# Decode attention with a gated feed-forward: one ordered load queue into five 32 KB slots, in place of two queues with their own buffers

## The chip, the cores and the metric

The kernel runs on one core of a Trainium2 chip. A core has five engines that each work through their own list of instructions: TensorE (PE, matrix products, with its weight loads shown apart as PEld), VectorE (DVE), ScalarE (ACT), GpSimd (POOL) and SyncE (SP, which here only starts transfers). They meet through semaphores. Data comes from the chip's memory (HBM) into SBUF (128 partitions) through 16 DMA engines that all queues share. PE writes into PSUM, eight banks of 2 KB per partition.

The metric is device time in microseconds (us), the median over several runs. Before the change it is 385.56 us, median of 3 runs (385.26 to 386.15).

## The reference, cut to what matters

One token (x, 512 values) goes through attention over a cache of 32,768 keys and through a feed-forward block, and the two results are mixed by a scalar gate.

```
q = x @ wq                                  # 512 -> 32 heads x 128
scores = einsum("bhqd,bhkd->bhqk", q, k) * Dh**-0.5   # k, v: 8 kv heads, each for 4 q heads
p = softmax(scores)                         # over 32768 keys
a = einsum("bhqk,bhkd->bhqd", p, v).reshape(1, 1, 4096) @ wo      # 4096 -> 512
b = (silu(x @ w_gate) * (x @ w_up)) @ w_down                      # 512 -> 1792 -> 512
g = sigmoid(sum(x * gate_w))
out = g * a + (1 - g) * b
```

All inputs are bfloat16. k_cache and v_cache hold 67.1 MB each, wq and wo 4.19 MB each, the three feed-forward matrices 1.84 MB each. Each byte is used once, and 148.11 MB are read in all.

## The kernel before, in words

Keys lie in the cache as rows of 128 values. PE turns 8 tiles of 128 keys into columns (a *fill*: 8 transposes against an identity, L474, into one of three PSUM tiles `pst`), DVE copies the fill to SBUF (L722, `ktT`), and PE multiplies each of the 8 tiles with the group's 4 query columns (*scores*, L443, three fills later, into `ps_sc`). A group is one kv head: 256 tiles, 32 fills. When a group's scores are there, DVE and POOL find the maximum (L706, L314) and ACT takes exponentials (L571) into `ET`, one of three group buffers. Then PE sums the values: one matmul per tile of 128 keys with the tile of V as the weights and 4 columns of `ET` moving (*PV*, L496, 256 per group into `ps_o`).

**Loads.** K comes in 64 blocks of 1 MB: 128 partitions with 32 rows of 256 bytes each, an 8 KB run of memory per partition. SP issues them (L341) into four slots of `kbuf`; each waits until PE has transposed the block that held the slot (`s_fill`). On the same queue, x, gate_w and wq come first (L320 to L322), the feed-forward matrices follow K blocks 3, 5 and 7 (L348), and wo follows K block 40 (L351). V also comes in 64 blocks of 1 MB, on ACT's queue (L609), into eight slots of `vbuf` and, later, four in the space of wq (`wqo`). ACT issues each at a place in its own program that `v_thr` works out, between the exponentials. So two queues share the DMA engines.

**PE's order** is the list `jobs`: from group 1 on, K blocks of group g alternate with V blocks of group g-1; a K block is four times (8 transposes, 8 scores), a V block is 32 PV matmuls in a row. The feed-forward's products (L394 with a strided view of the weights, L407) and the query product (L379) are inserted by number of fill.

**The end.** The last group's PV is followed by a sum of the exponentials over partitions (L512), reciprocal, scaling, a transpose within DVE and a permutation by matmul (L747 to L756, L521), 128 matmuls with wo (L528), the mix (L758, L763), four transposes of the result into one row (L538), a cast (L772) and the store of 512 values as one row (L357).

Of the kernel before, what the change touches and what calls it, by code (L numbers as in the profile page):

```python
# [5 lines left out]
ACT = mybir.ActivationFunctionType  # L6
# [7 lines left out]
def bass_gated_mix__gqa_block_cached__swiglu_ffn__decode_kernel(  # L14
# [14 lines left out]
    Hkv = A_k_cache.shape[1]  # L29
# [3 lines left out]
    HPG = H // Hkv  # L33
    F = B_w_gate.shape[1]
    NOUT = A_wo.shape[1]
    assert DH == 128 and D % 128 == 0 and F % 128 == 0 and HPG == 4 and NOUT % 128 == 0
    assert H == 32, "wo blocked layout / permutation assumes 32 q heads of 128"
    KC = D // 128
    FC = F // 128
    OC = NOUT // 128  # L40
    G = Hkv
    assert G >= 3
    R = 32
    B = 128 * R
    assert S % B == 0
    NB = S // B
    NT = NB * R
    TPF = 8
    FPB = R // TPF
    FPG = NB * FPB  # L50
    NF = G * FPG
    TPSB = 512 // HPG
    FPSB = TPSB // TPF
    NSB = G * NT // TPSB
    assert NT % TPSB == 0 and (NT // TPSB) == 2
    NKB = 4
    NVB = NB
    NVX = 4
    NVT = NVB + NVX
    VI_EXT = NB  # L60
# [5 lines left out]
    VLAG = 3  # L66
    WOJ = H * DH // 128
    SCALE = float(DH) ** -0.5

    J_FFN = FPG + 2  # L70
    J_ACT_SG = J_FFN + 6
    J_DVE_T = J_ACT_SG + 4
    J_OUTB = J_DVE_T + 8
    J_BCOL = J_OUTB + 3
    assert J_BCOL + LAG + NST < 2 * FPG, "ffn chain must complete inside group 1"

    def sb_thr(f):
        return min(NF - 1, FPSB * f + FPSB - 1 + LAG + 1)

    def exp_thr(g):  # L80
        return sb_thr(2 * g + 1)

    act_busy = set()
    for g in range(G):
        t0 = exp_thr(g)
        for j in range(t0 + 1, t0 + 11):
            act_busy.add(j)

    def copier(j):
        if j in act_busy:  # L90
            return "D"
        return "D"

    cp_index = []
    nd = na = 0
    for j in range(NF):
        if copier(j) == "D":
            nd += 1
            cp_index.append(("D", nd))
        else:  # L100
            na += 1
            cp_index.append(("A", na))

    jobs = []
    for g in range(G):
        kj = [("K", g, b) for b in range(NB)]
        vj = [("V", g - 1, b) for b in range(NB)] if g >= 1 else []
        seq = kj[:VLAG] if g >= 1 else kj[:]
        ki = len(seq)
        vi = 0  # L110
        turn_v = True
        while ki < len(kj) or vi < len(vj):
            if turn_v and vi < len(vj):
                seq.append(vj[vi])
                vi += 1
            elif ki < len(kj):
                seq.append(kj[ki])
                ki += 1
            else:
                seq.append(vj[vi])  # L120
                vi += 1
            turn_v = not turn_v
        jobs += seq
    jobs += [("V", G - 1, b) for b in range(NB)]
    assert len(jobs) == 2 * G * NB

    NVALL = G * NB
    vslot = [0] * NVALL
    vprev = [-1] * NVALL
    _occ = {}  # L130
    for vi in range(NVALL):
        allowed = range(NVT) if vi >= VI_EXT else range(NVB)
        free = [sl for sl in allowed if sl not in _occ]
        if free:
            sl = free[0]
        else:
            sl = min(allowed, key=lambda x: _occ[x])
            vprev[vi] = _occ[sl]
        vslot[vi] = sl
        _occ[sl] = vi  # L140

    with ExitStack() as es:
        def S_(name):
            return es.enter_context(nc.semaphore(name))

        sem_k_load = [S_(f"s_k_load{i}") for i in range(NKB)]
        sem_v_load = [S_(f"s_v_load{i}") for i in range(NVT)]
        sem_fill = S_("s_fill")
        sem_kt_free = S_("s_kt_free")
        sem_v_free = S_("s_v_free")  # L150
        sem_cp_d = S_("s_cp_d")
        sem_cp_a = S_("s_cp_a")
        sem_ld_x = S_("s_ld_x")
        sem_ld_wq = S_("s_ld_wq")
        sem_ld_wf = S_("s_ld_wf")
        sem_ld_wo = S_("s_ld_wo")
        sem_out = S_("s_out")
        sem_const = S_("s_const")
# [4 lines left out]
        sem_dve_pm = S_("s_dve_pm")  # L163
        sem_pe_x = S_("s_pe_x")
        sem_pe_q = S_("s_pe_q")
        sem_pe_h = S_("s_pe_h")
# [4 lines left out]
        sem_pe_fin = S_("s_pe_fin")  # L171
        sem_dve_x = S_("s_dve_x")
        sem_dve_prod = S_("s_dve_prod")
        sem_dve_gpart = S_("s_dve_gpart")
        sem_dve_qT = S_("s_dve_qT")
        sem_dve_t1 = S_("s_dve_t1")
        sem_dve_tT = S_("s_dve_tT")
        sem_dve_bcol = S_("s_dve_bcol")
        sem_pmax = S_("s_pmax")
        sem_dve_esum2 = S_("s_dve_esum2")  # L180
        sem_dve_rS = S_("s_dve_rS")
        sem_dve_oT1 = S_("s_dve_oT1")
        sem_dve_oT2 = S_("s_dve_oT2")
        sem_dve_O2 = S_("s_dve_O2")
        sem_dve_diff = S_("s_dve_diff")
        sem_dve_res = S_("s_dve_res")
        sem_dve_row = S_("s_dve_row")
        sem_act_g = S_("s_act_g")
        sem_act_sg = S_("s_act_sg")
# [611 lines left out]
```

## Time and profile before

| what | value |
|---|---|
| median of the runs (lowest, highest) | 385.56 us (385.26, 386.15) |
| span of the profiled execution, first to last instruction | 384.1 us |
| mean granted clock of TensorE | 0.746 |
| PE busy; weight loads | 298.7 us (78%); 293.3 us (76%), 6583 instructions each |
| DVE busy | 188.1 us (49%) |
| ACT busy | 30.4 us (8%) |
| read from HBM | 148.11 MB, 386 GB/s over the span |
| K and everything else on SP's queue | 81.01 MB, 51.0% of the 16 DMA engines |
| V on ACT's queue | 67.11 MB, 42.7% |
| instruction fetches on queue q8 | 51 packets, 0.84 MB, 0.9% |

The profiled execution spans 384.1 us, 1.5 us below the median of the runs; a run also has what lies around the instructions. The page gives busy time by engine, the same in 40 slices of 9.6 us, the DMA queues, the chain of work that ended last, and the costliest groups of instructions. In the profile, "issue" as the releaser of a wait means that the engine waited for nothing that the profile shows: no semaphore, no operand. Queue q1 is SP's, q10 ACT's, and q8 carries the instructions of the engines themselves from memory.

### The profile page before, as it was taken

What the parts mean: (1) busy time and instruction counts of PE and PEld (TensorE: products, weight loads), DVE (VectorE), ACT (ScalarE), POOL (GpSimd) and SP (SyncE); (2) the same over time, 40 slices, a digit from 0 to 9 for tenths busy, and PEclk for the clock granted to TensorE, in tenths of its full rate; (3) what the DMA queues carried; (4) which work ended last, traced back from release to release, by engine and by line L of the source; (5) the groups of instructions that cost most, each with busy time, mean ns of one, the idle gap of its engine ahead of it and who ended that gap; (6) DMA issues with size and microseconds to landing.
All of it is one profiled execution on the core that took longest, in us unless ns stands there. A gap on an engine that the chain in (4) does not pass through costs nothing.

```text
span 384.1 us, 14171 instructions
## 1 busy us (share of the span) xinstructions
PE 298.7 (78%) x6583; PEld 293.3 (76%) x6583; DVE 188.1 (49%) x305; ACT 30.4 (8%) x142; POOL 4.5 (1%) x19
## 2 busy tenths in 40 slices
PE   0592644899779797989997893278898888888895
PEld 0592644899779797989997893278898888887885
DVE  0291523427447464765575553155447653755502
ACT  1000000140003100300030002000003000300030
POOL 0000000000000000000000000000000000000000
PEclk9996656659787868595669885588668887788855
DMA  7999999989998999999999999999999999999810
GB/s 307 398 422 418 420 423 418 385 339 426 414 417 315 381 417 418 418 419 413 418 417 419 415 434 421 411 420 418 416 419 420 411 418 418 404 422 417 357 72 2
DMA packets 19215, 149.01 MB, mean 388 GB/s; under 512 B 2131, under 2 KB 2134, under 8 KB 2134
## 3 DMA queue, kind: packets, MB, share of 16 engines
q1 hardware_dynamic: 9942, 81.01, 51.0%
q10 hardware_dynamic: 9216, 67.11, 42.7%
q8 instruction: 51, 0.84, 0.9%
q14 instruction: 6, 0.05, 0.0%
HBM read 148.11 MB, written 0.00 MB: 386 GB/s over the span
## 4 chain that ended last, share of the span: by engine, by line
PE 46%; DMA 40%; issue 13%; DVE 1%; ACT 0%; SPq 0%; POOLq 0%; POOL 0%; ACTq 0%
DMA kbuf<-in_A_k_cache_dram 36%; PE pst L474 26%; PE ps_o L496 8%; PE ps_sc L443 7%; DMA wqo<-in_A_wq_dram 3%; PE ps_m L394 2%; PE ps_m L528 1%; PE ps_m L379 1%; PE ps_m L407 0%; ACT ET L571 0%; DVE ktT L722 0%; DVE res_row L772 0%; DVE pmaxf L706 0%; PE pst L538 0%; PE pst L512 0%
## 5 line engine op out<-in xcount | busy, mean ns | idle before, releaser
L722 DVE COPY ktT<-pst 128x1024 bf16<-128x1024 bf16 x256 | 172.9, 691 | 160.1 <-PE pst L474 159.0
L474 PE MATMUL pst<-ident,kbuf 128*128 128x128 bf16 x2048 | 208.2, 264 | 52.1 <-DMA kbuf<-in_A_k_cache_dram 49.8
L474 PEld LDWEIGHTS pst<-ident,kbuf 128*128 128x128 bf16 x2048 | 157.3, 118 | 55.5 <-DMA kbuf<-in_A_k_cache_dram 52.0
L443 PE MATMUL ps_sc<-qT,ktT 128*128 128x4 bf16 x2048 | 95.2, 168 | 2.8 <-issue 2.5
L443 PEld LDWEIGHTS ps_sc<-qT,ktT 128*128 128x128 bf16 x2048 | 92.0, 105 | 3.3 <-issue 2.7
L496 PE MATMUL ps_o<-ET,vbuf 128*128 128x4 bf16 x1408 | 42.7, 168 | 7.9 <-issue 7.9
L496 PEld LDWEIGHTS ps_o<-ET,vbuf 128*128 128x128 bf16 x1408 | 40.0, 98 | 8.4 <-issue 8.3
L561 ACT ACTIVATE nbias<-gmax 128x4 f32<-128x4 f32 x8 | 1.6, 206 | 316.3 <-POOL gmax L314 316.3
L571 ACT ACTIVATE ET<-ps_sc,nbias 128x128 bf16<-128x128 f32 x64 | 22.5, 377 | 0.2
L496 PE MATMUL ps_o<-ET,wqo 128*128 128x4 bf16 x640 | 19.0, 168 | 3.0 <-issue 2.3
L496 PEld LDWEIGHTS ps_o<-ET,wqo 128*128 128x128 bf16 x640 | 18.0, 98 | 3.2 <-issue 2.4
L571 ACT ACTIVATION_READ_ACCUMULATOR ET<-ps_sc,nbias 128x1 f32 x64 | 13.8, 216 | 0.0
L379 PE MATMUL ps_m<-xT,wqo 128*128 128x1 bf16 x128 | 3.5, 165 | 11.0 <-DMA wqo<-in_A_wq_dram 11.0
L379 PEld LDWEIGHTS ps_m<-xT,wqo 128*128 128x128 bf16 x128 | 3.5, 104 | 11.1 <-issue 11.1
L706 DVE TENSOR_REDUCE pmaxf<-ps_sc 128x4 f32<-128x512 f32 x16 | 10.9, 681 | 0.4 <-PE ps_sc L443 0.4
L314 POOL PARTITION_ALL_REDUCE gmax<-pmax x8 | 3.0, 373 | 340.2 <-DVE pmax L710 340.2
L394 PE MATMUL ps_m<-xT,wfo 128*128 128x1 bf16 x112 | 6.9, 198 | 0.0
L394 PEld LDWEIGHTS ps_m<-xT,wfo 128*128 128x128 bf16 x112 | 6.8, 166 | 0.0
L661 DVE TENSOR_SCALAR kq<-kf 128x1 f32<-128x1 f32 x3 | 0.5, 153 | 8.6 <-POOL kf L300 8.5
L528 PE MATMUL ps_m<-O,wfo 128*128 128x1 bf16 x128 | 3.7, 165 | 0.4 <-DVE O L756 0.3
L528 PEld LDWEIGHTS ps_m<-O,wfo 128*128 128x128 bf16 x128 | 3.6, 104 | 0.6 <-DVE O L756 0.4
L747 DVE RECIPROCAL rS<-pst 128x32 f32<-128x32 f32 x1 | 0.4, 359 | 6.3 <-PE pst L512 6.3
(50 smaller groups left out, 19.7 us busy)
## 6 DMA issues: line engine op xcount, KB each, us to landing
kbuf<-in_A_k_cache_dram SPq DMA_DIRECT2D x64, 1024.0 KB, 16.1
vbuf<-in_A_v_cache_dram ACTq DMA_DIRECT2D x44, 1024.0 KB, 23.9
wqo<-in_A_v_cache_dram ACTq DMA_DIRECT2D x20, 1024.0 KB, 22.4
wqo<-in_A_wq_dram SPq DMA_DIRECT2D x1, 4096.0 KB, 12.3
wfo<-in_A_wo_dram SPq DMA_DIRECT2D x1, 4096.0 KB, 28.2
wfo<-in_B_w_gate_dram SPq DMA_DIRECT2D x1, 1792.0 KB, 27.2
wfo<-in_B_w_up_dram SPq DMA_DIRECT2D x1, 1792.0 KB, 23.8
wfo<-in_B_w_down_dram SPq DMA_DIRECT2D x1, 1792.0 KB, 36.2
```

The costliest lines, as they stand in the source:

```text
L314: pool.partition_all_reduce(gmax[:, g, :], pmax[:, g, :], 128, ReduceOp.max).then_inc(sem_gmax, 1)
L379: ins = pe.matmul(ps_m[:, M_Q0 + h : M_Q0 + h + 1], wq_v[:, c, h * DH : (h + 1) * DH], xT[:, c : c + 1], start=(c == 0), stop=(c == KC - 1),)
L394: ins = pe.matmul(ps_m[:, base + j : base + j + 1], wt[:, c, :].rearrange("d (p j) -> d j p", j=FC)[:, j, :], xT[:, c : c + 1], start=(c = ...
L443: ins = pe.matmul(bank[:, col : col + HPG], ktT[:, slot, t * 128 : (t + 1) * 128], qT[:, g * HPG : (g + 1) * HPG], start=True, stop=True,)
L474: ins = pe.transpose(stb[:, t * 128 : (t + 1) * 128], kbuf[:, slot, r, :], ident[:, :],)
L496: ins = pe.matmul(ps_o[:, g * HPG : (g + 1) * HPG], vsl[:, r, :], ET[:, g % NEG, :, n], start=(n == 0), stop=(n == NT - 1),)
L528: ins = pe.matmul(ps_m[:, M_A0 + oc : M_A0 + oc + 1], wo_v[:, j, oc * 128 : (oc + 1) * 128], O2[:, j : j + 1], start=(j == 0), stop=(j == ...
L561: act.activation(nbias[:, g, :], gmax[:, g, :], ACT.Copy, scale=-SCALE).then_inc(sem_nbias, 1)
L571: act.activation(ET[:, g % NEG, h, bk * TPSB : (bk + 1) * TPSB], sc[:, h, :], ACT.Exp, bias=nbias[:, g, h : h + 1], scale=SCALE, accum_out ...
L661: dchain(dve.tensor_scalar(kq[:, i : i + 1], kf[:, :], thr, None, op0=ALU.is_ge))
L706: dve.tensor_reduce(pmaxf[:, f, :], sc, AX.X, ALU.max).then_inc(sem_pmax, 1)
L722: dve.tensor_copy(ktT[:, j % NKT, :], pst[j % NST][:, :]).then_inc(sem_cp_d, 1)
```

## The change

All large loads now go through SP's queue alone, in the order of one list, `stream`: wq, K half 0 of group 0, w_gate and w_up, K half 1, w_down, K half 0 of group 1 and V half 0 of group 0, and so on in pairs, V being one group behind; the last two V halves and wo close the list. An entry takes one of five slots of 32 KB per partition (`ring`), and is issued when the entry five places before it has been used up. K and V now come in halves of a group, 4 MB at a time, with one 32 KB run of memory per partition. The last V half is cut into pieces of 2 MB, 1 MB and two of 512 KB, wo into pieces of the same sizes. x and gate_w are loaded as columns by two small transfers on ACT's queue, and ACT issues nothing else.

PE follows `pe_work`. From K half 1 of group 1 on, each K half is worked together with the V half before it in sixteen equal parts: 8 transposes, 8 scores, 8 PV. The gate's sum over partitions is a matmul in place of a POOL reduction. At the end, the sum of the exponentials stands before the last V half. The wo products run over its 32 row blocks outermost and four result columns inside, with a strided view of wo, into four PSUM banks, so they can begin with the first piece. The result is mixed in one DVE operation and stored from 128 partitions with 4 values each. The four transposes, the cast and two of the DVE steps are gone.

The core of the diff:

```diff
-    jobs = []
-    for g in range(G):
-        kj = [("K", g, b) for b in range(NB)]
-        vj = [("V", g - 1, b) for b in range(NB)] if g >= 1 else []
...
+    RH = S // 256
+    SLOT = RH * DH
+    NSLOT = 5
+    FPH = RH // TPF
+    V_LAST = (64, 32, 16, 16)
+    WO_CUT = (16, 8, 4, 4)
+    stream = [("wq",), ("K", 0, 0), ("F1",), ("K", 0, 1), ("F2",)]
+    for g in range(1, G):
+        for hf in range(2):
+            stream += [("K", g, hf), ("V", g - 1, hf)]
+    stream += [("V", G - 1, 0), ("V", G - 1, 1), ("wo",)]
...
-                for kind, g, b in [j for j in jobs if j[0] == "K"]:
-                    slot = ki % NKB
-                    if ki >= NKB:
-                        sp.wait_ge(sem_fill, FPB * (ki - NKB + 1))
-                    sp.dma_start(
-                        kbuf[:, slot, :, :],
...
+                for i, e in enumerate(stream):
+                    if i >= NSLOT:
+                        sp.wait_ge(*released[stream[i - NSLOT]])
...
+                        kind, g, hf = e
+                        src = (A_k_cache if kind == "K" else A_v_cache)[
+                            0, g, hf * (S // 2) : (hf + 1) * (S // 2), :
+                        ].rearrange("(p r) d -> p r d", r=RH)
+                        dst = kv_slot(e)
...
+                            sp.dma_start(dst, src).then_inc(sem_ld[i], 16)
...
+                        pe.wait_ge(load_sem(e), 16)
+                        f = 2 * g + hf
+                        if v is not None:
+                            pe.wait_ge(load_sem(("V",) + v), 16)
+                            pe.wait_ge(sem_exp, 2 * HPG * v[0] + HPG * (v[1] + 1))
+                        for q in range(FPH):
+                            j = f * FPH + q
+                            emit_fill(j, kv_slot(e), q)
+                            if scored <= j - LAG:
+                                emit_scores(scored)
+                                scored += 1
+                            if v is not None:
+                                n = RH // FPH
+                                emit_pv(v[0], v[1], kv_slot(("V",) + v), q * n, n, q == FPH - 1)
...
-                for oc in range(OC):
-                    for j in range(WOJ):
-                        ins = pe.matmul(
-                            ps_m[:, M_A0 + oc : M_A0 + oc + 1],
-                            wo_v[:, j, oc * 128 : (oc + 1) * 128],
...
+                for c, n in enumerate(WO_CUT):
+                    pe.wait_ge(sem_ldo[c], 16)
+                    for j in range(j0, j0 + n):
+                        for oc in range(OC):
+                            ins = pe.matmul(
+                                ps_a[:, oc, :],
+                                wo_v[:, j, :].rearrange("p (n c) -> p c n", c=OC)[:, oc, :],
...
-                act.dma_start(
-                    vslot_ap(slot),
-                    A_v_cache[0, g, b * B : (b + 1) * B, :].rearrange(
-                        "(p r) d -> p r d", r=R
-                    ),
-                ).then_inc(sem_v_load[slot], 16)
...
-                dve.tensor_tensor(
-                    diff_col[:, :], ps_m[:, M_A0 : M_A0 + OC], b_col[:, :], ALU.subtract
-                ).then_inc(sem_dve_diff, 1)
...
+                sp.dma_start(
+                    out[0, 0, :].rearrange("(p c) -> p c", c=OC), res[:, :]
+                ).then_inc(sem_out, 16)
```

Where the instructions stand. On PE, in the middle of group 1, the kernel before has one V block between K blocks (each row: line, operation, result and operands, shape, what it waits for; `kbuf` and `vbuf` are the K and V slots, `pst` the transposed tiles):

```order
L496 MATMUL ps_o<-ET,vbuf 128x4 [waits s_v_load2]
L496 MATMUL ps_o<-ET,vbuf 128x4 x31
L474 MATMUL pst<-ident,kbuf 128x128 [waits s_cp_d,s_k_load1]
L474 MATMUL pst<-ident,kbuf 128x128 x7
L443 MATMUL ps_sc<-qT,ktT 128x4 [waits s_cp_d]
L443 MATMUL ps_sc<-qT,ktT 128x4 x7
L474 MATMUL pst<-ident,kbuf 128x128 [waits s_cp_d]
L474 MATMUL pst<-ident,kbuf 128x128 x7
```

The changed kernel at the start of one of its thirteen pairs of halves (`ring` holds K and V, `ps` is the whole of PSUM; `s_ld18` and `s_ld19` are the loads of the two halves):

```order
L344 MATMUL ps<-ident,ring 128x128 [waits s_exp,s_cp,s_ld18,s_ld19]
L344 MATMUL ps<-ident,ring 128x128 x7
L359 MATMUL ps<-qT,ktT 128x4 [waits s_cp]
L359 MATMUL ps<-qT,ktT 128x4 x7
L371 MATMUL ps<-ET,ring 128x4 x8
L344 MATMUL ps<-ident,ring 128x128 [waits s_cp]
```

The 32 PV matmuls that stood in a row are spread eight by eight behind the fills, and one wait at the head of a pair stands for both loads and the exponentials.

On SP's queue, the middle and the end before:

```order
L341 DMA kbuf<-in_A_k_cache_dram 128x4096 [waits s_fill] x33
L351 DMA wfo<-in_A_wo_dram 128x16384 [waits s_pe_b]
L341 DMA kbuf<-in_A_k_cache_dram 128x4096 [waits s_fill] x23
L357 DMA out_dram<-res_row 1x512 [waits s_dve_row]
```

and the last fills of the queue in the changed kernel:

```order
L283 DMA ring<-in_A_k_cache_dram 128x16384 [waits s_pv]
L283 DMA ring<-in_A_v_cache_dram 128x16384 [waits s_fill]
L283 DMA ring<-in_A_v_cache_dram 128x16384 [waits s_pv]
L278 DMA ring<-in_A_v_cache_dram 128x8192 [waits s_fill]
L278 DMA ring<-in_A_v_cache_dram 128x4096
L278 DMA ring<-in_A_v_cache_dram 128x2048 x2
L265 DMA ring<-in_A_wo_dram 128x8192 [waits s_pv]
L265 DMA ring<-in_A_wo_dram 128x4096
L265 DMA ring<-in_A_wo_dram 128x2048 x2
L285 DMA out_dram<-res 128x4 [waits s_res]
```

V has moved into SP's queue, wo from the middle to the end, and each load waits for a whole half that was used up.

In all, PE has 6571 matrix products where it had 6582, SP issues 43 loads and one store where it issued 71 loads and one, and ACT 2 where it issued 64.

More of the change, by code (lines that the diff above doesn't have):

```diff
@@ L124, in bass_gated_mix__gqa_block_cached__swiglu_ffn__decode_kernel @@
[L124 to L140, printed above, removed]
+    V_LAST = (64, 32, 16, 16)
@@ L535, in _ @@
[L535 to L545 removed]
+                pe.wait_ge(sem_O2, 1)
+                j0 = 0
@@ L560, in emit_exps @@
+                act.wait_ge(sem_pe_h, 1)
+                act.activation(sg[:, :], ps_m[:, M_G0 : M_G0 + FC], ACT.Sigmoid).then_inc(
+                    sem_sg, 1
+                )
+                for g in range(G):
                     act.wait_ge(sem_gmax, g + 1)
```

733 lines of the change are left out of this document (276 added, 457 removed).

## The prediction

> **What bounds the kernel now.** I read the page's busy lines first, then the rate of the transfers over the span, the busy time by stretch, the waits of PE, and the chain at the end.
>
> ```profile
> span 384.1 us, 14171 instructions
> PE 298.7 (78%) x6583; PEld 293.3 (76%) x6583; DVE 188.1 (49%) x305; ACT 30.4 (8%) x142; POOL 4.5 (1%) x19
> GB/s 307 398 422 418 420 423 418 385 339 426 414 417 315 381 417 418 418 419 413 418 417 419 415 434 421 411 420 418 416 419 420 411 418 418 404 422 417 357 72 2
> ```
>
> From 19 us to 355 us the transfers run at about 418 GB/s, with dips near 80 and 120 us. At that rate 148.1 MB take 354 us; the other 30 us are the start, the dips and a tail that hardly loads. PE is close behind, as the stretches show (length, PE busy and its instructions, PEld, DVE, ACT, POOL, granted clock, share of the DMA engines, GB/s):
>
> ```profile
> 100.00:150.00 50.00, 43.69 (x1016) 43.40 (x1017) 28.02 (x44) 4.39 (x18) 0.37 (x1) 0.76 0.97 390
> 150.00:200.00 50.00, 46.17 (x963) 45.49 (x963) 28.33 (x44) 4.50 (x25) 0.74 (x2) 0.66 1.01 418
> 260.00:350.00 90.00, 76.93 (x1686) 75.23 (x1685) 50.33 (x77) 6.22 (x34) 0.74 (x2) 0.78 1.01 417
> 370.00:384.10 14.10, 9.85 (x312) 9.12 (x308) 2.02 (x7) 0.00 (x0) 0.00 (x0) 0.50 0.01 2
> ```
>
> What PE waits for differs. First from 100 to 200 us, then from 260 to 360:
>
> ```profile
> PE ps_o L496 <- issue: 7.7, 4, 2.3
> PE ps_m L407 <- issue: 2.1, 1, 2.1
> ```
>
> ```profile
> PE pst L474 <- DMA kbuf<-in_A_k_cache_dram: 13.1, 15, 1.5
> ```
>
> The second is a kernel bound by its loads. The first is not: PE stops for "issue" even in the middle of a V block, where no instruction has a semaphore:
>
> ```profile
> 128.62 0.81 PE L496 MATMUL ps_o<-ET,wqo 128*128 128x4 bf16 x25
> 131.76 0.33 PE L496 MATMUL ps_o<-ET,wqo 128*128 128x4 bf16 x7 [2.33 <-issue]
> ```
>
> What can it want there? Its next instructions. Queue q8 carries them, here over 100 to 200 us, and then from 364 to 374 when loads had nearly stopped:
>
> ```profile
> q10 hardware_dynamic: 2620, 19.04, 46.5%
> q8 instruction: 16, 0.26, 1.1%
> ```
>
> ```profile
> 364.00:374.00 10.00, 9.05 (x328) 8.91 (x329) 1.12 (x4) 3.11 (x17) 0.37 (x1) 0.62 0.22 87
> q8 instruction: 3, 0.05, 1.9%
> ```
>
> Over the whole span the queue has
>
> ```profile
> q8 instruction: 51, 0.84, 0.9%
> ```
>
> A fetch brings 16 KB. 13,166 PE and PEld instructions stand against 51 fetches: 258 for each, all other engines counted in. From 100 to 200 us PE ran 3959 of them, 15.5 fetches, so one each 6.45 us, with PE stalled; from 364 on, one each 3.3 us. So under full load PE gets 256 instructions per about 6.4 us, and that is hardly faster than the loads feed it. This second bound is what the forecast turns on.
>
> **The change part by part.**
>
> *Larger runs.* An 8 KB packet takes 46.5% of 1600 engine-us over 2324 full packets (19.04 MB), 0.32 us at most. The 32 KB packets of wq stand at 4 to 12 us:
>
> ```profile
> q1 hardware_dynamic: 106, 3.47, 101.4%
> 1.40 12.33 DMA wqo<-in_A_wq_dram
> ```
>
> That is 1.22 us each and 434 GB/s. I take 430 for all loads against 418 now. From above 434 bounds it, from below 418. The change makes no load busier in bytes, so at 430 the 134.2 + 5.5 + 4.2 MB after wq need 334.7 us, and the last would land at 13.7 + 334.7 = 348.4.
>
> [...]
>
> *PE's work in a pair.* A pair is 16 fills of 8 transposes, 8 scores and 8 PV: 384 matmuls, 768 instructions with the weight loads, three fetches. Its own time follows from the clock:
>
> ```profile
> 90.00 0.47 PE pst L474 x8
> 90.64 0.85 PE ps_o L496 x32
> 132.09 0.87 PE pst L474 x8
> 133.15 0.88 PE pst L474 x8
> ```
>
> At half clock transposes and scores of a fill start 1.06 us apart (132.09 to 133.15), at full clock 0.64 (90.00 to 90.64); 8 PV are a quarter of 0.85, 0.21. A pair is 16 x 1.27 = 20.4 us at half clock, 16 x 0.85 = 13.7 at full. The loads need 8.39 MB / 0.430 = 19.5. Clocks of 0.66 to 0.78 above, with PE at work 85 to 92% of the time, show that stalls bring the half clock; I take it for all the pairs.
>
> *Fetches beside 32 KB packets.* [...] The nearest rows: 6.4 us per fetch behind 8 KB packets, 3.3 with little load. From below: no more than now, 6.4, or down to 6.1 as one load queue is gone. From above: the whole excess of 3.1 us grows with the packet (1.22/0.32 = 3.8 times), 15 us. Between: a fetch meets a packet under way, half of 1.22 or 0.61 us, where it now meets half of 0.32 and at times a whole one of the other queue, 0.32 in the middle. That adds 0.3: 6.7 us. [...] Three fetches are 20.1 us, close to the 20.4 of half clock; as the two do not fit exactly into each other I take 20.6 for a pair. Each 0.1 us more per fetch costs 13 x 3 = 39 fetches, and three after them, 4.2 us.
>
> Three rows bear on what else is queued now: SP's waits, DVE's copies, and the query product.
>
> ```profile
> SPq L341 <- PE pst L474: 316.7, 60, 16.4
> L722 DVE COPY ktT<-pst 128x1024 bf16<-128x1024 bf16 x256 | 172.9, 691 | 160.1 <-PE pst L474 159.0
> L379 PE MATMUL ps_m<-xT,wqo 128*128 128x1 bf16 x128 | 3.5, 165 | 11.0 <-DMA wqo<-in_A_wq_dram 11.0
> ```
>
> *One list, one wait for both halves.* The first pair starts when K half 1 of group 1 has landed: 13.7 + 26.48 MB / 0.430 = 75.3 us. The three K halves alone before it, 16 x 0.64 x 3 = 31 us, with the query and feed-forward products (3.5, 6.9 and about 2), fit between, at full clock; at half clock 51 us would not, and the pairs would begin up to 8 us later. A pair of halves is given back only when it is done, while three more slots load: 12.6 MB, 29.3 us. A pair of 20.6 leaves 8.7 to spare, so SP's waits (60 on transposes before, 316.7 us in all, at no cost) cost nothing at first; when PE has fallen behind by more than that, the loads pause, but PE sets the end then.
>
> *DVE, ACT, POOL.* DVE copies the same 256 fills, 172.9 us of copies in 384; in a pair 16 x 0.69 = 11 of 20. It hides as before. ACT loses 64 issues and is 92% idle. POOL loses one reduction. Nothing.
>
> *The end.*
>
> ```profile
> 371.44 3.59 PE ps_o L496 x128
> 375.04 0.49 PE pst L512 x2
> 375.94 0.20 DVE oTs L750
> 376.93 3.44 PE ps_m L528 x123
> 380.98 0.23 DVE res_col L763
> 382.59 0.27 SPq L357 DMA_DIRECT2D out_dram<-res_row  x1
> L394 PE MATMUL ps_m<-xT,wfo 128*128 128x1 bf16 x112 | 6.9, 198 | 0.0
> L528 PE MATMUL ps_m<-O,wfo 128*128 128x1 bf16 x128 | 3.7, 165 | 0.4 <-DVE O L756 0.3
> ```
>
> After the pairs come 3 x 128 PV, one fetch each: 3.6 us by the row without loads, 6.7 under load; I take 5.5, 16.5 in all. Scaling to permutation take 375.94 to 376.93, 1.0; L512 now stands earlier. wo's 128 matmuls read strided weights: 3.7 us as in L528, or, at L394's 6.9 for 112, 7.9. I take 5.5. Its pieces would land by 350 to 360 and are not waited for. Then 0.23 for the mix and 1.5 for the store (382.59 to 384.1). Gone are L758, L538 and L772: 380.79 to 382.59 without the mix, 1.6 us.
>
> *Sum.* 75.3 + 13 x 20.6 = 343.1; + 16.5 = 359.6; + 1.0 + 5.5 + 0.2 + 1.5 = 367.8 as a span, against 384.1. The median of the runs was 1.5 above the span: **369.3 us**, 4.2% faster. Its own range is 360 (full clock in part) to 382 (7.0 us per fetch).
>
> **The rivals.**
>
> *Fetches cost nothing.* They are hidden, and PE follows the loads: last V lands at 338.6, wo at 348.4, PE ends a pair behind the last V pieces, some 5 us, and with wo's strided products and the store about 357.5, **359 us**. For it: from 260 to 360 PE waits for loads 13.1 us and for nothing else. Against it: 9.8 us of issue from 100 to 200.
>
> [...]
>
> *Fetches wait for a further whole packet, and it gets slower.* If an engine serves one more 32 KB packet before a fetch, the excess grows by 0.3 + 0.6 us, to 7.6 us. A pair is then 22.8 us: 39 x 0.9 + 3 x 0.9 = 38 us more than forecast; as the loads then pause and some fetches meet quiet engines, I give back 7: **400 us**. It decides from 7.1 us per fetch on, where 369.3 + 4 x 4.2 passes 385.6. For it: a fetch already takes 3.1 us longer under load than without, ten 8 KB packets, so it waits more than once. Against it: one queue fewer in the line.
>
> *No change.* At 7.0 to 7.1 us per fetch the gain is just eaten: **385 us**.
>
> *Larger runs are no faster.* At 418 GB/s the first pair starts at 77.1, 1.8 later, and PE sets the rest: **371 us**. For it: 417 is already near 434; against it: wq's row.
>
> **How the numbers follow.** Forecast 0.44, hidden fetches 0.17, runs no faster 0.05, no change 0.04, slower through fetches 0.24, and 0.06 for more than 8 us per fetch (above 415). The likeliest gives 369.3. For 8 in 10 the range goes from 356, below the hidden fetches, to 410, past the further packet. A measurement of this kernel tells about 0.2% from no change: faster 0.44 + 0.17 + 0.05 = 0.66, the same 0.04, slower 0.24 + 0.06 = 0.30.
>
> **What would show it.** In the changed profile: K and V loads at 428 to 434 GB/s between 20 and 75 us if the larger runs are right. The starts of the pairs, the first transposes behind a wait for two loads, 20 to 21 us apart; 19.5 with PE waiting for the ring is the rival of hidden fetches, over 22 with "issue" as the releaser and the loads pausing late in the span that of the further packet. One fetch per 6.5 to 6.9 us on q8. The wo products at 43 ns each and no transposes behind them. The prediction is wrong if pairs run at full clock (near 14 us and waiting for loads), if fetches exceed 7.1 us, or if the first pair starts past 80 us.

## The result and the profile after

The changed kernel takes 370.22 us, median of 4 runs (367.79 to 370.93), against 385.57 (385.26 to 386.15) for the one before: 0.959 of it, 95% interval 0.9555 to 0.9626. The forecast was 369.3. Where a run of a kernel lies more than 1.5% above its fastest, the ratio and its interval leave it out, while the median and the range take all four.

The runs of the change are not all alike: the one of 367.79 had a mean granted clock of 0.664, the three others 0.581 to 0.594. The profile is of the run of 370.93, with 0.594.

The page after, its first lines, clock and rate in 40 slices of 9.2 us:

```profile
span 369.1 us, 13987 instructions
PE 328.9 (89%) x6573; PEld 328.0 (89%) x6573; DVE 189.3 (51%) x302; ACT 27.8 (8%) x140; POOL 4.1 (1%) x17
PEclk9999768966755555555555555555555555555555
GB/s 327 398 418 433 419 456 423 421 439 408 446 424 430 418 426 431 442 415 431 428 423 421 411 433 385 444 414 414 392 423 429 430 417 392 423 421 408 379 251 2
```

The transfers now hold about 428 GB/s for the first half, with no dips. In the second half they fall a little (418 GB/s from 180 to 260 us, 413 from 260 to 345), and the clock stands at 0.50 from the second pair to the end. Busy time by stretch, before (first fence) and after (second), in the columns of the prediction, shows where the time came from:

```profile
14.00:100.00 86.00, 62.41 (x1230) 61.66 (x1227) 39.98 (x63) 6.07 (x21) 0.79 (x2) 0.74 0.99 406
100.00:130.00 30.00, 26.56 (x635) 26.35 (x636) 16.62 (x27) 4.39 (x18) 0.37 (x1) 0.77 0.94 372
360.00:370.00 10.00, 9.13 (x266) 8.96 (x265) 3.81 (x7) 3.11 (x17) 0.37 (x1) 0.67 0.58 225
```

```profile
14.00:100.00 86.00, 69.36 (x1477) 68.97 (x1478) 47.84 (x86) 4.74 (x20) 0.39 (x1) 0.82 1.01 429
100.00:180.00 80.00, 80.00 (x1497) 80.00 (x1495) 45.64 (x69) 6.21 (x34) 0.74 (x2) 0.50 1.00 429
260.00:345.00 85.00, 85.00 (x1632) 84.96 (x1630) 48.57 (x74) 6.20 (x34) 0.85 (x3) 0.50 0.99 413
345.00:356.00 11.00, 7.02 (x243) 6.86 (x240) 0.55 (x2) 3.11 (x17) 0.26 (x1) 0.50 0.98 381
356.00:369.10 13.10, 7.49 (x230) 7.22 (x230) 0.82 (x4) 0.00 (x0) 0.00 (x0) 0.50 0.06 20
```

Loading ends near 356 us in place of 370, and what follows it takes 13.1 us in place of 14.1: 14 of the 15 us are won by the time the loads end. Before, the loads lost time in the dips up to 130 us and in the half-empty stretch from 360 to 370.

The three largest of PE's waits over the whole span, and then the starts of the first two pairs:

```profile
PE ps L297 <- DMA gwT<-in_gate_w_dram: 24.9, 1, 24.9
PE ps L344 <- DMA ring<-in_A_k_cache_dram: 5.0, 2, 3.6
PE ps L371 <- issue: 4.8, 2, 2.8
```

```profile
77.44 1.04 PE L344 MATMUL ps<-ident,ring 128*128 128x128 bf16 x8 [3.58 <-DMA ring<-in_A_k_cache_dram]
97.20 1.04 PE L344 MATMUL ps<-ident,ring 128*128 128x128 bf16 x8 [1.41 <-DMA ring<-in_A_k_cache_dram]
```

The end of the last pair and what follows it, from the chain of waits:

```profile
340.56 0.87 PE ps L344 x8
341.84 0.87 PE ps L344 x8
343.12 0.75 PE ps L359 x24
...
348.06 2.85 issue
...
354.86 1.94 issue
356.81 2.87 PE ps L371 x101
...
360.76 4.44 PE ps L443 x128
```

PE starts a fill each 1.28 us (340.56 to 341.84), and from the start of the second pair to 343 us it does not stop: twelve pairs of 20.48 us. So the pair's length came out as forecast, by the prediction's term for PE's own work at half clock (20.4 us); fetches and loads both hide behind it. The first pair is different, though its instructions stand in the same order:

```profile
77.40:90.00 12.60, 12.56 (x233) 12.57 (x233) 6.82 (x11) 0.00 (x0) 0.00 (x0) 0.51 0.99 425
90.00:96.00 6.00, 5.65 (x158) 5.48 (x154) 4.71 (x7) 0.00 (x0) 0.00 (x0) 1.00 0.98 418
97.00:343.00 246.00, 245.80 (x4609) 245.81 (x4610) 139.89 (x210) 18.62 (x102) 2.22 (x6) 0.50 1.00 421
```

It begins at half clock, behind the wait of 3.58 us. At 90.2 us the clock rises to full, with no stop and no change in the work, and a fill then takes 0.86 us. So PE gets ahead of the loads, waits 1.41 us for the second pair, and from there on the clock is at half. The two waits for issue come only afterwards, when PV alone asks for 256 instructions in 3.5 us.

This left three questions: why does the clock stay at half from the second pair on, when PE never rests and the first pair left it; how far away are the other two limits; and which part of the change made the loads better.

### The profile page after: what moved, and what is told of

Same layout as the page of the kernel before. It is cut to its first block, busy times and chain, and to the rows that moved or that the text cites. A ratio compares the mean times of both kernels' runs of the same rounds, so it can differ in the third digit from the quotient of the medians.

```text
span 369.1 us, 13987 instructions
## 1 busy us (share of the span) xinstructions
PE 328.9 (89%) x6573; PEld 328.0 (89%) x6573; DVE 189.3 (51%) x302; ACT 27.8 (8%) x140; POOL 4.1 (1%) x17
## 4 chain that ended last, share of the span: by engine, by line
PE 81%; DMA 16%; issue 2%; DVE 0%; ACTq 0%; DVEq 0%
PE ps L344 50%; PE ps L371 14%; PE ps L359 12%; DMA ring<-in_A_k_cache_dram 10%; DMA gwT<-in_gate_w_dram 6%; PE ps L316 2%; PE ps L443 1%; PE ps L297 1%; PE ps L330 1%; PE ps L416 0%; PE ps L307 0%; ACTq L455 0%; PE ps L434 0%; DVE res L591 0%; DVE O2a L585 0%
## 5 line engine op out<-in xcount | busy, mean ns | idle before, releaser
L344 PE MATMUL ps<-ident,ring 128*128 128x128 bf16 x2048 | 242.0, 294 | 5.0 <-DMA ring<-in_A_k_cache_dram 5.0
L563 DVE COPY ktT<-ps 128x1024 bf16<-128x1024 bf16 x256 | 175.1, 691 | 129.0 <-PE ps L344 128.8
L344 PEld LDWEIGHTS ps<-ident,ring 128*128 128x128 bf16 x2048 | 184.6, 132 | 5.2 <-DMA ring<-in_A_k_cache_dram 5.2
L359 PEld LDWEIGHTS ps<-qT,ktT 128*128 128x128 bf16 x2048 | 101.7, 112 | 0.5 <-issue 0.4
L359 PE MATMUL ps<-qT,ktT 128*128 128x4 bf16 x2048 | 99.7, 171 | 0.3 <-issue 0.3
L371 PE MATMUL ps<-ET,ring 128*128 128x4 bf16 x2048 | 84.9, 168 | 4.9 <-issue 4.8
L371 PEld LDWEIGHTS ps<-ET,ring 128*128 128x128 bf16 x2048 | 71.3, 103 | 5.2 <-issue 5.2
L297 PE MATMUL ps<-xT,ring 128*128 128x1 bf16 x128 | 3.6, 166 | 24.9 <-DMA gwT<-in_gate_w_dram 24.9
L297 PEld LDWEIGHTS ps<-xT,ring 128*128 128x128 bf16 x128 | 3.5, 104 | 24.9 <-DMA gwT<-in_gate_w_dram 24.9
L481 ACT ACTIVATE ET<-ps,nbias 128x128 bf16<-128x128 f32 x64 | 22.5, 376 | 0.2
L481 ACT ACTIVATION_READ_ACCUMULATOR ET<-ps,nbias 128x1 f32 x64 | 13.8, 216 | 0.0
L500 DVE TENSOR_TENSOR prod_col<-xT,gwT 128x4 f32<-128x4 bf16 x1 | 0.2, 163 | 24.9 <-DMA gwT<-in_gate_w_dram 24.9
L551 DVE TENSOR_REDUCE pmaxf<-ps 128x4 f32<-128x512 f32 x16 | 10.9, 681 | 0.5 <-PE ps L359 0.5
```

Of the source, the lines that this page charges most:

```text
L297: ins = pe.matmul(ps_m[:, M_Q0 + h : M_Q0 + h + 1], wq_v[:, c, h * DH : (h + 1) * DH], xT[:, c : c + 1], start=(c == 0), stop=(c == KC - 1),)
L344: ins = pe.transpose(stb[:, t * 128 : (t + 1) * 128], src[:, q * TPF + t, :], ident[:, :])
L359: ins = pe.matmul(ps_sc[f % NSC][:, col : col + HPG], ktT[:, j % NKT, t * 128 : (t + 1) * 128], qT[:, g * HPG : (g + 1) * HPG], start=True ...
L371: ins = pe.matmul(ps_o[:, g * HPG : (g + 1) * HPG], src[:, r, :], ET[:, g % NEG, :, k], start=(k == 0), stop=(k == NT - 1),)
L481: act.activation(ET[:, g % NEG, h, hf * RH : (hf + 1) * RH], sc[:, h, :], ACT.Exp, bias=nbias[:, g, h : h + 1], scale=SCALE, accum_out=esu ...
L551: dve.tensor_reduce(pmaxf[:, f, :], sc, AX.X, ALU.max).then_inc(sem_pmax, 1)
```

## Experiments on the clock

**PV in blocks of 32.** The same instructions, with PV behind every fourth fill.

```diff
-                            if v is not None:
-                                n = RH // FPH
-                                emit_pv(v[0], v[1], kv_slot(("V",) + v), q * n, n, q == FPH - 1)
+                            if v is not None and q % 4 == 3:
+                                n = 4 * RH // FPH
+                                emit_pv(v[0], v[1], kv_slot(("V",) + v), (q - 3) * TPF, n, q == FPH - 1)
```

> The changed kernel, with PV in blocks of 32 after every fourth fill instead of 8 after each. The same instructions, loads and waits. Theory 'clock': a pair takes 20.48 us since PE stays at half clock, and it stays there because the PV matmuls between the fills thin the transposes out (8 in 1.28 us); in four fills without PV they come every 1.06 us, the clock can rise, pairs fall to what loads or fetches allow, 19.5 to 20 us: 357 to 364 us. Theory 'fetch' (the prediction's 6.7 us for 256 instructions sets the pair): order is of no matter, 20.1 to 20.5 us for a pair, 366 to 371 us with waits for issue in place of busy time.

Measured: 367.11 us (365.87 to 367.66), ratio 0.9539 (0.950 to 0.9578). As a total that lies in the range of the theory 'fetch', and its interval still touches that of the change. The stretch 78 to 330 us, in the change and here, and PE's waits here tell more:

```profile
78.00:330.00 252.00, 250.45 (x4743) 250.29 (x4741) 144.43 (x217) 18.62 (x102) 2.22 (x6) 0.51 1.00 422
```

```profile
78.00:330.00 252.00, 220.79 (x4852) 217.79 (x4850) 146.16 (x222) 18.67 (x102) 2.22 (x6) 0.73 1.00 427
PE ps L344 <- DMA ring<-in_A_k_cache_dram: 16.1, 12, 3.8
PE ps L371 <- issue: 9.6, 7, 2.6
PE ps L344 <- issue: 8.3, 7, 2.2
```

The clock rises from 0.51 to 0.73, though nothing but the order differs. The other runs agree: over the span the mean clock is 0.75 to 0.77 in the four of this kernel, 0.58 to 0.66 in those of the change. What is gained turns into waits for loads (16.1 us, 5.0 in the change) and for issue (17.9 us, 4.8 in the change). So the clock is one limit, with the other two close behind it.

**Ten transposes in a fill.** More work, of the one kind that moves 128 columns.

```diff
-                    for t in range(TPF):
+                    again = 2 if j >= 3 * FPH else 0
+                    for t in list(range(again)) + list(range(TPF)):
```

> The changed kernel with more work: from the fourth half on, each fill's first two transposes are done twice (10 transposes, 8 scores, 8 PV; same result). If the half clock stays, a fill takes 1.28 + 0.22 = 1.50 us, a pair 24.0, and 13 pairs cost 45 us more: 414 us. Theory 'fetch' at 6.7 us each: 832 instructions are 3.25 fetches, 21.8 us for a pair, 386 us at full clock. [...]

Measured: 378.24 us (374.44 to 382.15), ratio 0.9753 (0.9694 to 0.9813); the ratio is that of the two shorter runs, 374.44 and 375.95, and the profile is of the longest. Neither forecast, 414 or 386, is met. The stretch, and two stops in the timeline of PE (other work stands between them):

```profile
78.00:330.00 252.00, 220.11 (x4924) 217.28 (x4921) 137.97 (x208) 18.66 (x102) 2.22 (x6) 0.81 0.98 409
```

```profile
184.29 0.33 PE L345 MATMUL ps<-ident,ring 128*128 128x128 bf16 x3 [1.38 <-issue]
...
190.79 0.45 PE L345 MATMUL ps<-ident,ring 128*128 128x128 bf16 x5 [0.36 <-issue]
```

The clock is at 0.81 although PE carries out 4% more instructions. The transposes stand more thickly here: 10 in 1.49 us at half clock (186.04 to 187.53), 6.7 in a us, against 8 in 1.28 us, 6.25 in a us, in the change; in the rows of fills without PV of the run before, at 0.73, they are 8 in 1.07 us (157.90 to 158.97), 7.5 in a us. And the time is then set mostly by fetches: of PE's waits, 40 us are for issue and 4.2 for loads of K and V. PE stops inside a row of transposes, here 6.5 us apart (184.29 to 190.79), with 128 matrix products and as many weight loads between, 256 instructions. Over the stretch 9845 instructions are 38.5 fetches, 6.55 us each.

**Scores twice.** To price a fetch at half clock.

```diff
-                    for t in range(TPF):
+                    for t in (2 if j >= 3 * FPH else 1) * list(range(TPF)):
                         col = (q * TPF + t) * HPG
```

> The changed kernel with each score matmul done twice from the fourth half on: 8 transposes, 16 scores, 8 PV in a fill, 1024 instructions or four fetches in a pair; same result. It prices a fetch under 32 KB load. At half clock a pair is 16 x 1.49 = 23.9 us if a fetch takes under 5.9 us and stays hidden: 414 us. At the prediction's 6.7 us it is 26.8 us: 452 us, with waits for issue. At 7.6 us 30.4 us: 498 us.

Measured: 422.51 us (418.22 to 424.99), ratio 1.0913. The clock stays at half, 0.51 over the longer stretch; the added scores stand between the transposes, 8 in 1.49 us (89.22 to 90.71) where the change has 8 in 1.28. From 78 to 120 us, under full load, and over the longer stretch:

```profile
78.00:120.00 42.00, 36.92 (x815) 36.50 (x812) 19.26 (x30) 3.10 (x17) 0.37 (x1) 0.57 0.99 415
78.00:330.00 252.00, 244.22 (x5235) 243.33 (x5233) 121.02 (x181) 15.52 (x85) 1.85 (x5) 0.51 0.86 356
```

1627 instructions in 42 us are again one fetch in 6.6 us, with PE idle for 5 us. Over the longer stretch PE is so slow that the loads pause (356 GB/s), and with one fetch in 6.16 us it hardly stops any more (2.7 us idle from 120 to 330 us): a fetch takes no more than that here, where it took 6.6 us at 415 GB/s. That is why 422 lies nearer to the expectation for hidden fetches (414) than to that for 6.7 us (452).

**What this shows of the clock.** The order has an effect, but it does not settle the matter. The run with 8 KB loads (next section) has the PE order of the change, and there the clock rises again and again in the middle of a pair, at 168.6 us for instance:

```profile
159.60:168.60 9.00, 8.97 (x169) 8.98 (x170) 4.96 (x8) 0.00 (x0) 0.00 (x0) 0.52 1.01 419
168.60:176.70 8.10, 7.97 (x222) 7.85 (x218) 6.32 (x10) 0.00 (x0) 0.00 (x0) 1.00 1.01 420
```

In the pairs of that run and of the change, each fall to half clock that lasts more than one fill stands right behind a stop of PE, of 0.9 us or longer (3.58 and 1.41 us in the change). Ahead of the pairs the change shows a fall without a stop: among 112 products of one moving column the clock is 1.00 from 40 to 42 us and 0.50 from 42 to 46.6. The rise comes later, while PE is busy: 5 to 30 us after the fall in the run with 8 KB loads, 12.8 us after it in the first pair of the change, 3 to 15 us in the kernels with PV in blocks of 32 and with ten transposes. With the scores done twice it does not come for longer than one fill from 84 us to the end of the pairs (0.50 in each stretch from 130 to 365 us). Why it did not come for 246 us in the change, with an order that rises elsewhere, is shown by no run.

## Experiments on the loads

**8 KB runs in the same order.** Each 4 MB load as four of 1 MB.

```diff
-                            sp.dma_start(dst, src).then_inc(sem_ld[i], 16)
+                            for c in range(4):
+                                rr = slice(c * RH // 4, (c + 1) * RH // 4)
+                                sp.dma_start(dst[:, rr, :], src[:, rr, :]).then_inc(sem_ld[i], 16)
...
```

> The changed kernel with each 4 MB load of K or V issued as four loads of 1 MB with 8 KB runs, in the same order on the same queue into the same slots. Theory 'larger runs carry the gain': loads fall back to 418 GB/s, the first pair starts 1.8 us later, a pair needs 20.1 us of loads; if that were the limit, 13 x 0.6 + 1.8 = 10 us slower, 380 us. Theory 'clock' (PE sets the pair at 20.48): about 371, 0 to 2 us slower, with the later start only.

Measured: 372.96 us (371.84 to 373.57), ratio 0.9692 (0.9653 to 0.9731), 0.7% above the change by the medians: near the theory 'clock' (0 to 2 us slower), far from the 380 of the other. With PV in blocks of 32 as well, the same question where the clock is not in the way:

> PV in blocks of 32 (as in the run before, 367.1 us) together with loads of 1 MB with 8 KB runs (as in the other, 373.0 us). It asks what larger runs are worth when PE is no longer held at half clock. Theory 'loads set the pair here': 418 in place of 428 GB/s is 0.5 us for each of 13 pairs and 2 us before them, 373 to 376 us, no faster than with 8 PV behind each fill. Theory 'fetch sets the pair, and 8 KB packets make fetches 0.2 to 0.3 us shorter': 362 to 368 us.

Measured: 371.95 us (371.22 to 373.73), ratio 0.9662 (0.9614 to 0.971), against 0.9539 for the blocks with 32 KB runs: between the two ranges, 1 us below that of the loads. Here are the stretch and PE's main wait of the first of the two:

```profile
78.00:330.00 252.00, 223.40 (x4731) 221.69 (x4729) 144.09 (x216) 18.67 (x102) 2.23 (x6) 0.66 1.01 418
PE ps L346 <- DMA ring<-in_A_k_cache_dram: 36.1, 15, 7.0
```

At 418 GB/s PE waits for the ring in each pair, and the order of PV brings no more than 1 us (371.95 against 372.96). So larger runs are worth 3 to 5 us: 427 to 429 GB/s against 418.

**Fetches beside 8 KB packets.** Ten transposes and 8 KB runs together, both edits as above.

> The run with 10 transposes in a fill (378.2 us, 3.25 fetches in a pair of 21.2 us on average, full clock in most of it, so 6.5 us for a fetch beside 32 KB packets) with the loads of 1 MB and 8 KB runs. It prices a fetch beside 8 KB packets. The prediction put it at 6.4 against 6.7 us, so a pair should be 1 us shorter, down to the loads' 20.1: 368 to 373 us. If the packet's size is of no matter to a fetch, 377 to 381 us.

Measured: 374.92 us (373.6 to 375.11), ratio 0.9737. Between the two ranges. The total does not set it apart from ten transposes beside 32 KB packets, as the two shorter runs of that kernel, 374.44 and 375.95, lie on both sides. The stretch:

```profile
78.00:330.00 252.00, 222.63 (x5145) 219.40 (x5143) 144.03 (x217) 18.67 (x102) 2.23 (x6) 0.85 1.01 418
```

10,288 instructions are 40.2 fetches, 6.27 us each, with PE waiting for the ring part of the time (25.5 us over the span); so a fetch takes at most 6.3 us beside 8 KB packets. I take two stops for issue within 8 us as one fetch apart, as those at 184.29 and 190.79 above are with their 256 instructions. Beside 8 KB packets these distances are 6.2 us here (three of them) and with PV in blocks of 32 (6.17 to 6.45, mean 6.23, seven). Beside 32 KB packets they are 6.15 to 6.47 with PV in blocks of 32 (mean 6.25, four) and 5.9 to 7.5 with ten transposes (mean 6.67, nine). So a fetch costs 6.2 to 6.7 us, and a step of 0.3 us for the size of the packet, as the prediction took it, is not shown.

**V on ScalarE's queue.** The same slots and 4 MB transfers, two queues.

```diff
+                    if e[0] == "V" and e != ("V", G - 1, 1):
+                        continue
                     if i >= NSLOT:
...
+                def load_v(g, hf):
+                    e = ("V", g, hf)
+                    i = place[e]
+                    act.wait_ge(*released[stream[i - NSLOT]])
+                    act.dma_start(
...
                 for g in range(G):
+                    load_v(g, 0)
+                    if g < G - 1:
+                        load_v(g, 1)
                     act.wait_ge(sem_gmax, g + 1)
```

> The changed kernel with the V halves (all but the last) issued on ScalarE's queue, with the same slots, releases and 4 MB transfers; ScalarE issues the two V loads of a group just before that group's exponentials. Two 32 KB queues then share the engines, K and V of a pair land together. If a fetch must wait for a packet of each queue (the mechanism of the rival at 7.6 us), pairs are 22.8 us and PE stops for issue: 395 to 405 us. If a fetch waits only for the packet under way, pairs stay at 20.5 us of half clock: 368 to 374, the later first pair included.

Measured: 393.31 us (391.83 to 395.98), ratio 1.0209 (1.0185 to 1.0234): slower than the kernel before. The number is near the one expected of fetches, but the reason isn't. PE's waits, then the issue of a V half on ACT's queue, the start of the pair that needs it, and the stretch around the issue:

```profile
PE ps L346 <- DMA ring<-in_A_k_cache_dram: 29.2, 9, 5.9
PE ps L361 <- issue: 8.7, 5, 2.6
PE ps L373 <- issue: 7.9, 5, 2.9
```

```profile
193.22 0.34 ACTq L467 DMA_DIRECT2D ring<-in_A_v_cache_dram  x1
```

```profile
216.56 1.03 PE L346 MATMUL ps<-ident,ring 128*128 128x128 bf16 x8 [2.48 <-DMA ring<-in_A_k_cache_dram]
```

```profile
186.00:194.00 8.00, 8.00 (x149) 8.00 (x148) 4.32 (x7) 0.00 (x0) 0.00 (x0) 0.50 0.37 156
78.00:330.00 252.00, 216.00 (x4297) 214.26 (x4298) 130.07 (x196) 15.55 (x85) 1.86 (x5) 0.59 0.93 386
```

A V half is issued when the last pair gives its slots back (193.22) and shares the engines with the K half that comes after it in the list and is issued 0.4 us later (193.62), so both land together, about 23 us later. Until the next slots come free nothing is left to load: the engines are 37% busy from 186 to 194 us. In the change's list V goes first, ahead of that K half, and the K half is loaded while PE works on the next pair. A pair takes about 22 us here, of which only a small part is stops for issue (18.8 us in the whole run), and the first pair starts at 83.38 us in place of 77.44, 6 of the 23 us. With these five slots the fixed order is what lets the loads run through (422 GB/s from 78 to 330 us in the change, 386 here).

**x and the gate first; the end in whole pieces.** Two parts of the change undone.

```diff
-                act.dma_start(xT[:, :], A_x[0, 0, :].rearrange("(p c) -> p c", c=KC)).then_inc(
+                sp.dma_start(xT[:, :], A_x[0, 0, :].rearrange("(p c) -> p c", c=KC)).then_inc(
...
```

> The changed kernel with the two small column loads of x and gate_w issued by SP ahead of wq, not by ScalarE beside it. In the profile of the change the second of them landed at 24.8 us and held the query product back by 11 us. Theory 'hidden': PE waits for the ring at the first pair (3.6 us) and the second (1.4 us) anyway, so the pairs start where they did, within 1 us of 370. Theory 'on the path': up to 5 us faster.

Measured: 369.92 us (369.26 to 371.22), ratio 0.9598 (0.9557 to 0.964). No difference, though PE's wait for the query product's operands ends at 14.2 us in place of 24.9: the first pair starts at 77.41 us (77.44 in the change), as PE waits for its loads anyhow.

```diff
-    V_LAST = (64, 32, 16, 16)
-    WO_CUT = (16, 8, 4, 4)
+    V_LAST = (128,)
+    WO_CUT = (32,)
```

> The changed kernel with the last V half and wo loaded whole (one transfer of 4 MB each), waits and order else the same. In the profile of the change PE reaches the last V half at 354 us and wo at 361, long after the pieces had landed. Theory 'PE is late at the end': 0 to 1 us slower. If the pieces are what lets the end overlap: last V whole lands 5 us later than its first half, and it gets 3 to 6 us slower.

Measured: 371.12 us (367.7 to 372.01), ratio 0.9609 (0.9552 to 0.9666). The shrinking pieces are worth nothing that can be measured, since PE comes to them late.

## A version with fewer and thicker instructions

If clock and fetches hold PE, PV is the place to change: with the exponentials of four key tiles as 16 columns of weights and four V tiles moving, 512 columns at once, 32 matmuls do what 128 did.

```diff
-                    for r in range(r0, r0 + n):
+                    for r in range(r0, r0 + n, 4):
                         k = hf * RH + r
                         ins = pe.matmul(
-                            ps_o[:, g * HPG : (g + 1) * HPG],
-                            src[:, r, :],
-                            ET[:, g % NEG, :, k],
+                            ps_pv,
+                            ET[:, g % NEG, k : k + 4, :].rearrange("p n h -> p (n h)"),
+                            src[:, r : r + 4, :],
...
+                    for i in range(4):
+                        ins = pe.matmul(
+                            ps_o[:, g * HPG : (g + 1) * HPG],
+                            oacc[:, i * 128 : (i + 1) * 128],
+                            ident[0:16, 4 * i : 4 * i + 4],
...
```

> The changed kernel with fewer and denser PV instructions: the exponentials of four key tiles (16 columns) are the weights, and the four V tiles (512 columns) move, 32 matmuls for a V half in place of 128; the 16 x 512 sums of a group are copied out by ScalarE and its four diagonal blocks added by four small matmuls. A pair has 576 instructions, 2.25 fetches or 14.9 us at the 6.6 us that the run with 10 transposes showed, and 16 x 1.07 = 17.2 us of PE at full clock. Theory 'fetch and clock together held PE back': both limits go, pairs fall to the loads' 19.5 us, PE waits for the ring in each, the end loses two or three fetch stalls: 355 to 361 us. If the half clock stayed, a fill would take 1.92 us and a pair 31: 500 us. If something else held the pair, 366 to 372.

Measured: 375.75 us (375.26 to 376.43), ratio 0.9747: slower than the change, and outside every range I had written. Clock and fetches are gone as limits, and still (the stretch, and from the chain a fill and the first V half after the pairs):

```profile
78.00:330.00 252.00, 251.94 (x3606) 161.84 (x3605) 145.51 (x218) 22.73 (x108) 2.23 (x6) 1.00 1.00 424
```

```profile
324.62 0.53 PE ps L377 x2
325.14 0.55 PE ps L348 x8
325.70 0.18 PE ps L363 x8
325.88 0.53 PE ps L377 x2
...
340.97 7.02 PE ps L377 x32
```

PE is busy all the time at full clock: a fill takes 1.26 us (324.62 to 325.88), as long as 1.28 at half clock before. Two wide matmuls take 0.53 us between other work, 32 in a row 0.22 each; the transposes behind them 0.55 in place of 0.47. So my price for the fill, 1.07 us, was too low; the excess stands where one kind of matmul follows the other. The pairs still end 2 us earlier than in the change (340.97 against 343.12). What makes the kernel slower is the end: each of the three V halves after the pairs now takes 7.0 us, 23 us with the sums copied out, where the change needs 16.6.

Next: eight wide matmuls in a row behind every fourth fill, and the last V half in single tiles.

> The wide PV of the run before (375.8 us), where a fill took 0.55 + 0.18 + 0.53 = 1.27 us at full clock, since each change between operations cost time; here eight wide matmuls stand together after every fourth fill, and the last V half is done in single tiles. Theory 'PE's own work set the pair there': 16 x 0.65 + 32 x 0.22 = 17.4 us for a pair, below the 19.5 us of the loads, so PE waits for the ring in each pair; wo lands near 350, and 4.4 us of products, the mix and the store follow: 355 to 360 us. If a pair stays at 20 us or more with PE busy, 365 to 370.

Measured: 364.5 us (364.21 to 364.93), ratio 0.9474 (0.946 to 0.9488). Pairs now wait for loads (20.7 us in 13 waits) as expected; the total missed its range because the end is longer:

```profile
78.00:330.00 252.00, 234.25 (x3678) 171.13 (x3676) 142.36 (x223) 22.73 (x108) 2.23 (x6) 0.98 1.00 429
PE ps L348 <- DMA ring<-in_A_k_cache_dram: 20.7, 13, 2.9
```

```profile
334.59 7.02 PE ps L387 x32
...
342.60 7.00 PE ps L387 x32
...
349.94 3.21 PE ps L377 x128
```

After the last pair (334.59), two wide V halves take 14 us, where single tiles take 3.2 to 3.5 each. So one more of them in single tiles:

> The wide kernel of the run before (364.5 us) with the second V half of group 6 also done in single tiles at the end, which takes 3.5 us where the wide form took 7.0, and its copy out moved before the last exponentials. Loads set the pairs there, but the end is PE's: 334.6 to 358.9 us. Theory 'the end is PE's own work': the last exponentials, ready about 339, hold the next V half for a little, so 2 to 3.5 us are gained: 361 to 362.5. If fetches for the 256 more instructions per half come late (6.5 us each), nothing is gained: 364 to 365.

Measured: 362.76 us (361.96 to 363.27), ratio 0.9419 (0.9376 to 0.9462), near what was expected. It beats both kernels, the changed one by about 2%.

## Why the prediction was right, and where it was not

**Larger runs, 430 GB/s.** Right: 429 in the first half, 418 with 8 KB runs, 3 to 5 us of the 15. The rival "no faster" was wrong about the runs, but its time (371) is near, since PE set the pairs.

**First pair at 75.3.** 77.44, behind a wait of 3.58 us for its loads. The prediction did not price the two small loads on ScalarE's queue at all: the second took 23.7 us beside wq, and the query product started only at 24.9 us. With both ahead of wq the pairs began at the same time, so this is hidden. Why the loads were 2 us later than forecast, at a rate of 428 to 431 GB/s, is not shown.

**A pair of 20.6 us.** 20.48, twelve times, and 19.8 for the first: 265.7 for 13 against 267.8. The term that sets it, PE's own work at half clock, is the forecast's. The reason that I gave for it, "stalls bring the half clock", was not shown by the rows I took it from: the clock is 0.66 where PE works 92% of the time and 0.76 where it works 87%. It fits the falls in the pairs only, which stand behind the waits of 3.58 and 1.41 us. I took it that stalls are also what keeps the half clock, and that is wrong: for 246 us there were none, and the clock stayed at 0.50. That it stayed for all twelve pairs is luck for the number. The same order went back to full clock in the first pair, and in the run with 8 KB loads in every pair or two (mean clock 0.66 from 78 to 330 us). At full clock a pair would have come down to the 19.6 us of the loads and of three fetches, at best some 10 us less for the twelve (an estimate from 428 GB/s and 6.55 us for a fetch). The run of 367.79, with its higher mean clock of 0.664, fits this.

**Fetches, 6.7 us.** Mis-sized by little, and not what set the time: 6.2 to 6.7 us in the runs, 6.55 on the mean with ten transposes. The 0.3 us for half a packet under way, an estimate of mine, is shown by no run: between two stops it is 6.4 to 6.6 us in the kernel before, with two queues of 8 KB packets (100.58 to 113.42, 150.84 to 157.31, 170.00 to 176.59), 6.2 beside one such queue, and 6.2 to 6.7 beside 32 KB packets. At half clock PE asks for one each 6.83 us (20.48 / 3), so they are hidden, by 0.1 to 0.6 us. The prediction's 4.2 us for each 0.1 us holds only beyond 6.83; below it nothing changes. By these figures the change would have lost its 15.4 us at 7.2 us per fetch (an estimate), where the prediction had 7.1. Its price with little load, 3.3 us, was no price: from 364 to 374 us, before the change, PE hardly stopped for issue (0.2 us), and its 657 instructions in 10 us are one fetch in 3.9 us, so a fetch took that or less.

**The rivals.** "Fetches cost nothing" is half right: they cost nothing in the pairs (no stop for issue from 97 to 343 us), but PE does not follow the loads, since the clock takes their place. "A further whole packet", 7.6 us, is the mean of no run; the kernel with two queues, 393 us, came near that rival's 400, for another reason.

**The list and its five slots.** The prediction let this part cost nothing. It does better than that: with the same slots and two queues the kernel loses 23 us. I had looked at what PE's lag would do to the loads, and not at what the order within the 12.6 MB of lead does.

**The end.** V after the pairs 16.6 us (343.12 to 359.68), forecast 16.5; wo's products 4.44, forecast 5.5; from the last of DVE's steps to the end of the span 3.5 (365.56 to 369.1), forecast 1.5. The two misses cancel in part (1.1 us less, 2.0 more), as the first pair (2.1 more) and the pairs together (2.1 less) cancel by chance. That the wo pieces would not be waited for was right, and with it that cutting them brings nothing.

## What to carry to other kernels

When three limits lie within 5% of each other, price each of them alone: removing one shows the next and little else (the wide PV freed clock and fetches, and its own changes of shape and its longer end took the gain back). Look at the granted clock beside the busy time: a PE that was 100% busy at 0.50 was sped up by the order of its instructions (0.73 and 367.11 us with PV in blocks of 32, against 0.51 and 370.22), and one wait of 1.41 us was followed by 246 us at half clock. With few large slots, put the loads into one queue in the order of use; two queues that shared the engines delivered late what was needed first (393 us against 370).

## What was not expected of the hardware

- PE at 100% busy for 246 us with the clock at 0.50, behind a wait of 1.41 us, where the same order had risen to full clock in the pair before; and a clock of 0.81 with ten transposes in a fill, where it was 0.51 with eight.
- Two loads of 8 bytes per partition on a second queue took 14.0 and 23.7 us while the 32 KB packets of wq and what follows it filled the engines.
- At full clock, with the wide PV, a matmul took longer where one kind followed another: transposes 0.55 us for eight behind wide matmuls, 0.47 otherwise; wide matmuls 0.27 us each in twos, 0.22 in a row of 32.
